# Gate logit as one more column of K's folded weight, and the skip diagonal made from the broadcast row

## Chip, cores and metric

The kernel runs on one core of one Trainium2 chip. The metric is device time in microseconds (us), the median of several executions. The kernel before was run three times: 148.78, 149.03 and 149.26 us, so its median is 149.03 us.

## What is computed

Two branches read the same input x (2048 tokens of 512 channels, bf16) and are mixed by a gate, one number a token. Branch A is a diagonal complex state-space recurrence of 512 states plus a skip term `x * Dskip`. Branch B is linear attention with 32 heads of 16 channels, whose features are softmaxes of a projected query or key and of its negative.

```python
    x = A_x
    g = _sigmoid((x * gate_w).sum(-1, keepdims=True))
    a = _A_ref(x, A_Lambda_re, A_Lambda_im, A_B_re, A_B_im, A_C_re, A_C_im, A_log_dt, A_Dskip)
    b = _B_ref(x, B_wqkv, B_w_phi, B_wo)
    return g * a + (1 - g) * b
...
        y = 2.0 * jnp.einsum("blp,dp->bld", hseq, Cmat).real + x * Dskip[None, None, :]
...
        pk = jnp.einsum("bhsd,hdf->bhsf", k, w_phi)
        phi_k = jnp.concatenate([_softmax(pk, axis=-1), _softmax(-pk, axis=-1)], axis=-1)
        kv = jnp.einsum("bhsf,bhsd->bhfd", phi_k, v)
```

## The kernel before

**The order of the work is written by hand.** Every stage is a generator (`st_k`, `st_a`, ...), and the list `ORDER` names them in turn: one token runs one generator up to its next `yield`. `@` gives the PSUM banks that a stage takes, `:D` gives an evacuation to the vector engine (DVE) in place of the scalar engine (ACT). Each engine then runs its own instructions in the order in which the tokens issued them, and a semaphore wait holds everything that stands behind it on that engine. So a token's place in the list is its place in the queue of every engine that it uses, GpSimd (POOL) and the DMA-issuing SP included.

**The prologue.** POOL makes a bf16 identity `ident`, issues the DMAs of the three parameter vectors into `vec_n` (L164), and makes an f32 identity `identf`, from which DVE builds masks (L283 to L288) and the block-diagonal `BD` of the feature weights (`st_B`, tokens `B`). TensorE (PE) transposes K's weight into `WTk` (`st_W`) and multiplies it by `BD`: that is the fold, `f0` to `f3`, one for each 128 input channels. Its evacuation writes K's folded weight `Wk2`, 480 columns (8 groups of 4 heads, 15 features a head: the first feature is the reference and stands as a zero). The products of a token tile with it (`k0` to `k15`, four matmuls each, L493) are evacuated by ACT into `Xq`, whose row for a tile is 8 groups of 64 elements, the first four of each zeroed by POOL (L279, L499).

**The parameters.** `V` transposes `vec_n` on PE and DVE casts it into `vec`. From there a long run of small DVE and ACT operations (tokens `U`, `P`, `M`) makes the recurrence's coefficients `dgs`. The last of them, `M2` (L421 to L429), runs on POOL: three of its operations and two in place (L424, L425) give the coefficients `S_NBI` and `S_BR`, L426 gives `S_NBR`, and L427 to L429 give powers of the decay. The stage `c` (L446 or L444, `C2<-CT,dgs`) multiplies the transposed C by these coefficients, on DVE for most tokens. `V2` is a second transpose, of `vec_m` (Dskip and gate_w, loaded by POOL at L281): DVE casts it into `vec`, POOL's `affine_select` (L339) makes from it the skip diagonal `Dd`, and `gw` makes a bf16 copy of gate_w, `gw_b`, on DVE (L398).

**The middle.** For each of five groups of token tiles DVE makes maxima, minima, differences and sums of features (`x`, `n`, `s`), ACT the exponentials (`e`), and PE accumulates the attention state (`a0` to `a4`, `st_a`). In the same `st_a` PE computes the gate's logit: for each of 16 tiles four matmuls with one column of output, `gw_b` against the token tile, into the unused end of a PSUM accumulator (L631). At the same time the state-space stages `b`, `g`, `z`, `h`, `H`, `p` run on all engines.

**The end.** `G` reads the logits and makes `nge` and the gate `G` (L803 to L809). The queries' features (`X0` to `X3`, `S0` to `S3`) go through SP's transposing DMAs into `phT` (L613), and PE then does, tile by tile, `y` (state-space output, L875, with the skip term by `Dd` at L882), `o` (L894) and `t` (the output projection, L943). `Drow`, Dskip broadcast to all partitions, is loaded by SP at L261 (token `Ld`) and used by four tiles whose skip term DVE makes (L913).

Of the kernel before, what the change touches and what calls it, by code (L numbers as in the profile page):

```python
# [27 lines left out]
k4@3 i0 M k2 i0 i0 i0 M Lb k10 i2 M k6 n0 k4 k7@0 k7 i2 Lb k8@7 i1 i2 x0 i1 i1 k13@6 M2 k11@0 n0 i2 k8 i1 x1 n1 x1 D  # L28
n1 x1 b200@1 i2 i1 L i0:D x1 D c1:D n1 Lc Lc i3:D n1 k11 e0 b010@7 b010 c0:D x1 n1 i2:D b200 x2 s0 c0:D s0 k12@3 k12
x2 g200@2 g200 n2 c1 b100@0 s0 b100 x2 b001@5 n2 Lv b000@7 Lc i1 b000 b111@4 b111 x2 n2 s0 n2 g000@2 b001 s0 c3:D  # L30
b011@3 b101@7 e1 x2 n2 g000 g000 Lx g001@5 g001 x3 s1 v1@4 b011 c3 s0 c2:D c2:D c1:D k14@2 g010@3 g010 Lo e2 x3 n3 s1
k13 D v0@0 v1 s1 g011@1 x3 c3:D g011 x3 g001 g011 v0 e2 k15@0 g011 g010 c0:D Lq Lq g010 s1 n3 k14 w2@6 c3 s0 D k15 n3
a0@54 s2 a0 g011 x3 n3 g011 Ld g010 g201@2 b101 Ld n3 s1 w2 g010 z0 b201@1 b201 z0 b110@7 n4 s1 x4 g101@3 g201 l2:D s2
s2 x4 n4 e3 z0 z0 w1@6 w1 b110 g100@2 g100 g101 g101 g100 s2 s2 s2 g111@1 l2:D l2:D g111 n4 g110@0 g110 e3 g110 g111
# [44 lines left out]
def kernel(  # L79
# [69 lines left out]
    vec_m = const.tile([8, P], BF16, name="vec_m")  # L149
# [13 lines left out]
    for n, src in enumerate((A_Lambda_im, A_Lambda_re, A_log_dt)):  # L163
        nc.gpsimd.dma_start(out=vec_n[4 * n:4 * n + 4, :], in_=src.rearrange("(j p) -> j p", p=P))  # L164

# [6 lines left out]
    gw_b = const.tile([P, KT], BF16, name="gw_b")  # L172
# [15 lines left out]
    Xq = pR.tile([P, NTI, D], BF16, name="Xq")  # L188
# [18 lines left out]
    WTk = Xq[:, 12:16, :]  # L207
# [71 lines left out]
    nc.gpsimd.memset(Xq[:, 0:12, :].rearrange("p n (hh x) -> p n hh x", hh=8)[:, :, :, 0:4], 0.0)  # L279
    for n, src in enumerate((A_Dskip, gate_w)):  # L280
        nc.gpsimd.dma_start(out=vec_m[4 * n:4 * n + 4, :], in_=src.rearrange("(j p) -> j p", p=P))  # L281
# [52 lines left out]
    def st_V2():  # L334
        pvt = bank([P, 8], BF16, "pvt")
        nc.tensor.transpose(pvt[:], vec_m[:], ident[0:8, 0:8])
        yield
        nc.vector.tensor_copy(out=vec[:, 3:5, :].rearrange("p n j -> p (n j)"), in_=pvt[:])
        nc.gpsimd.affine_select(out=Dd[:], in_=dsk.unsqueeze(2).to_broadcast([P, KT, P]), compare_op=ALU.is_equal,  # L339
                                fill=0.0, base=0, pattern=[[0, KT], [-1, P]], channel_multiplier=1)  # L340
        yield
# [55 lines left out]
    def st_gw():  # L397
        nc.vector.tensor_copy(out=gw_b[:], in_=vec[:, 4, :])  # L398
        yield

# [47 lines left out]
    def fold(W2, WT, dtile):  # L448
        pf = bank([P, DF], F32, "pf")
        for j in range(KT):  # L450
            MM(out=pf[:, j * DF // KT:(j + 1) * DF // KT], lhsT=WT[:, j, dtile * P:(dtile + 1) * P], rhs=BD[:, j].rearrange("p g f -> p (g f)"), start=True, stop=True)
        yield
        evac(W2[:, dtile, :].rearrange("p (hh f hl) -> p hh f hl", hh=8, f=Dh - 1), pf[:].rearrange("p (hh hl f) -> p hh f hl", hh=8, hl=4))
        yield

    def st_f(d):
        return fold(Wk2, WTk, d)

    def st_w(d):
        return fold(Wq2, WTq, d)  # L460
# [34 lines left out]
    def xrel(n):  # L495
        return Xq[:, n, :].rearrange("p (hh x) -> p hh x", hh=8)[:, :, 4:]

    def xzero(n0, n1):
        nc.gpsimd.memset(Xq[:, n0:n1, :].rearrange("p n (hh x) -> p n hh x", hh=8)[:, :, :, 0:4], 0.0)  # L499
# [5 lines left out]
    def st_k(ti):  # L505
        pk = bank([P, DF], F32, "pk")
# [27 lines left out]
    def v5(ap3):  # L534
        return ap3.rearrange("p l (hh f hl) -> p l hh f hl", hh=8, f=Dh)
# [14 lines left out]
    def feat_max(p, first, L):  # L550
        X5 = v5(Xq[:, first:first + L, :])
# [3 lines left out]
        VT(out=half(EE, 0), in0=X5, in1=live["mx", p].to_broadcast([P, L, 8, Dh, 4]), op=ALU.subtract)  # L555
        yield

    def feat_min(p, first, L):
        X5 = v5(Xq[:, first:first + L, :])
        yield from tree(X5, L, ALU.min, "mn", ("mn", p))  # L560
        VT(out=half(live["EE", p], 1), in0=live["mn", p].to_broadcast([P, L, 8, Dh, 4]), in1=X5, op=ALU.subtract)  # L561
        yield
# [56 lines left out]
    def st_a(n):  # L619
        first, L = KGROUPS[n]  # L620
        for u in range(L):
            n_ = first + u
            ti = KO[n_]
# [6 lines left out]
            for kt in range(KT):  # L630
                MM(out=live["acc"][1][:, 4 * KVW + ti:4 * KVW + ti + 1], lhsT=xT[:, kt, ti * P:(ti + 1) * P],  # L631
                   rhs=gw_b[:, kt:kt + 1], start=False, stop=(n_ == NTI - 1 and kt == KT - 1), skip_group_check=True)
# [329 lines left out]
    st = {"V": st_V(), "V2": st_V2(), "U": st_U(), "P": st_P(), "P2": st_P2(), "P3": st_P3(), "P4": st_P4(), "B": st_B(), "gw": st_gw(),  # L962
# [60 lines left out]
```

## Time and profile before

| | |
|---|---|
| three runs | 148.78, 149.03, 149.26 us; median 149.03 us |
| profiled execution, first to last instruction | 147.2 us span |
| what the median has beyond that span | 1.8 us |
| busy: PE, DVE, ACT, POOL | 140.8, 135.1, 123.4, 45.4 us |
| granted TensorE clock | full speed in all 40 slices |

The page names one time of the profiled execution, its span; its own total is taken as the span and the 1.8 us that the median has around it. Times below are positions in that span. In a timeline row the columns are start, duration, engine, line, operation, output and inputs, size, and in brackets the idle time just before with what ended it. A duration on DVE and ACT reaches a little into the next instruction, so the cost of one in a dense run is the distance between starts. PE's ends are modelled, so there too starts are what is compared. A DMA row on POOL or SP is the issue, not the transfer.

### The profile page before, as it was taken

Reading aid. Unit: us, or ns where it says so; the run is one execution under the profiler, and the core shown is the slowest. Engines: PE = TensorE matmul, PEld = TensorE weight load, DVE = VectorE, ACT = ScalarE, POOL = GpSimd, SP = SyncE. Lnnn points to the kernel's source line nnn. Section 1 sums busy time; section 2 is a strip of 40 time slices with the busy share of each in tenths; the row PEclk is TensorE's granted clock in tenths of the full one; section 3 lists DMA queues with packets and bytes.
Section 4 is the critical chain, followed back from the end, with each engine's and each line's share of the span. In section 5 each row is a group of like instructions: output and inputs, shape, how many; then the busy total and the mean of one; then the engine's idle time right before and its main releaser. Section 6 shows DMA issues by size and latency. Waiting matters only on the chain.

```text
span 147.2 us, 2881 instructions
## 1 busy us (share of the span) xinstructions
PE 140.8 (96%) x1014; PEld 73.3 (50%) x1014; DVE 135.1 (92%) x330; ACT 123.4 (84%) x222; POOL 45.4 (31%) x61
## 2 busy tenths in 40 slices
PE   6999999999999999999999999999979999999990
PEld 2744444444544644554454656545445554545650
DVE  2879999999999999999999999999998999979740
ACT  3479999999999999999999999999988997912110
POOL 7503600003138195797545353051003003000000
PEclk9999999999999999999999999999999999999999
DMA  5999998990846586789878969969988999999643
GB/s 123 233 184 170 181 179 160 239 290 2 195 94 90 88 114 99 80 127 169 131 111 141 144 90 191 123 126 164 208 179 153 192 214 159 199 180 271 129 111 114
DMA packets 56047, 22.63 MB, mean 154 GB/s; under 512 B 44768, under 2 KB 54880, under 8 KB 56032
## 3 DMA queue, kind: packets, MB, share of 16 engines
q1 hardware_dynamic: 47584, 15.05, 52.7%
q0 software_dynamic: 7504, 7.09, 33.8%
q10 hardware_dynamic: 944, 0.31, 0.9%
q8 instruction: 8, 0.13, 0.4%
q14 instruction: 7, 0.06, 0.1%
HBM read 2.51 MB, written 2.10 MB: 31 GB/s over the span
## 4 chain that ended last, share of the span: by engine, by line
DVE 45%; PE 36%; ACT 9%; DMA 4%; issue 3%; DVEq 0%
PE PS L875 17%; PE PS L943 8%; DVE EE L597 6%; DVE mn L544 5%; DVE mx L544 5%; DMA phT<-EE 4%; DVE EE L555 4%; DVE sq L575 4%; DVE EE L561 3%; PE PS L894 3%; PE PS L493 3%; PE PS L324 2%; DVE w L723 2%; ACT vx L137 2%; ACT Xq L137 2%
## 5 line engine op out<-in xcount | busy, mean ns | idle before, releaser
L567 ACT ACTIVATE EE<-EE 128x2048 bf16<-128x2048 bf16 x16 | 30.3, 1933 | 0.4 <-DVE EE L561 0.4
L493 PE MATMUL PS<-WKV,xT 128*128 128x480 bf16 (+1 forms) x128 | 29.2, 372 | 0.2 <-ACT WKV L137 0.2
L493 PEld LDWEIGHTS <-xT 128*128 128x128 bf16 x192 | 18.1, 97 | 19.7 <-issue 0.9
L137 ACT CAST Xq<-PS 128x480 bf16<-128x480 f32 x32 | 17.5, 592 | 0.2
L653 PE MATMUL PS<-xT,BT 128*128 128x512 bf16 x64 | 16.2, 379 | 0.0
L875 PE MATMUL PS<-C,H 128*128 128x512 bf16 x64 | 15.6, 379 | 0.0
L943 PE MATMUL PS<-Wo,oT 128*128 128x512 bf16 (+2 forms) x68 | 15.5, 366 | 0.0
L493 PE MATMUL PS<-Wq,xT 128*128 128x480 bf16 x64 | 14.9, 365 | 0.0
L641 PE MATMUL PS<-xT,BT 128*128 128x512 bf16 x64 | 14.8, 379 | 0.0
L529 POOL DMA_DIRECT2D C<-CT x4 | 6.8, 1712 | 18.1 <-DVE CT L446 18.1
L907 DVE TENSOR_TENSOR on<-PS,rd 128x512 bf16<-128x512 f32 x16 | 10.9, 684 | 1.0 <-ACT rd L901 0.9
L529 POOL DMA_DIRECT2D eb<-dg x4 | 4.8, 1201 | 22.3 <-ACT dg L444 10.9
L949 ACT ACTIVATE ot<-PS,G 128x512 bf16<-128x512 f32 (+1 forms) x10 | 6.3, 647 | 4.7 <-PE PS L943 4.7
L641 PEld LDWEIGHTS <-BT 128*128 128x128 bf16 x64 | 6.3, 98 | 7.5
L561 DVE TENSOR_TENSOR EE<-mn,Xq 128x2048 bf16<-128x2048 bf16 (+1 forms) x9 | 9.9, 1095 | 0.0
L555 DVE TENSOR_TENSOR EE<-Xq,mx 128x2048 bf16<-128x2048 bf16 (+1 forms) x9 | 9.8, 1094 | 0.0
L575 DVE TENSOR_TENSOR sq<-EE 128x2048 bf16<-128x2048 bf16 (+1 forms) x9 | 9.8, 1094 | 0.0
L943 PEld LDWEIGHTS <-oT 128*128 128x128 bf16 x68 | 6.4, 98 | 6.7
L898 ACT ACTIVATE ld<-PS 128x32 f32<-128x32 f32 x16 | 3.0, 202 | 7.8 <-PE PS L894 7.8
L597 DVE TENSOR_TENSOR EE<-EE,rc 128x2048 bf16<-128x2048 bf16 x8 | 9.6, 1210 | 0.0
L653 PEld LDWEIGHTS <-BT 128*128 128x128 bf16 x64 | 6.1, 97 | 6.9 <-issue 0.2
L137 ACT CAST vx<-PS 128x512 bf16<-128x512 f32 x16 | 9.5, 618 | 0.0
(196 smaller groups left out, 329.7 us busy)
## 6 DMA issues: line engine op xcount, KB each, us to landing
out_dram<-ot SPq DMA_DIRECT2D x7, 256.0 KB, 2.5
C<-CT POOLq DMA_DIRECT2D x4, 256.0 KB, 5.2
eb<-CT POOLq DMA_DIRECT2D x4, 256.0 KB, 4.3
eb<-dg POOLq DMA_DIRECT2D x4, 256.0 KB, 4.3
sq<-sq POOLq DMA_DIRECT2D x3, 256.0 KB, 3.8
WKV<-in_B_wqkv_dram SPq DMA_DIRECT2D x1, 512.0 KB, 4.9
Wo<-in_B_wo_dram SPq DMA_DIRECT2D x1, 512.0 KB, 4.1
WKV<-in_A_x_dram SPq DMA_DIRECT2D x2, 256.0 KB, 4.8
```

The costliest lines, as they stand in the source:

```text
L137: nc.scalar.copy(out=out_ap, in_=in_ap)
L493: MM(out=pt[:], lhsT=xT[:, kt, ti * P:(ti + 1) * P], rhs=W[:, kt, :], start=(kt == 0), stop=(kt == KT - 1))
L544: VT(out=dst, in0=cur[:, :, :, 0:n, :], in1=cur[:, :, :, n:2 * n, :], op=op)
L555: VT(out=half(EE, 0), in0=X5, in1=live["mx", p].to_broadcast([P, L, 8, Dh, 4]), op=ALU.subtract)
L561: VT(out=half(live["EE", p], 1), in0=live["mn", p].to_broadcast([P, L, 8, Dh, 4]), in1=X5, op=ALU.subtract)
L567: aexp(out=EE[:, l_:l_ + 2], in_=EE[:, l_:l_ + 2], func=ACT.Exp)
L575: VT(out=sq.rearrange("p q x i -> p x q i"), in0=e4[:, :, 0:2], in1=e4[:, :, 2:4], op=ALU.add)
L597: VT(out=E5[:, u:u + 2], in0=E5[:, u:u + 2], in1=rc[:, u:u + 2].to_broadcast([P, 2, 2 * NB, Dh, 4]), op=ALU.mult)
L641: MM(out=pb[:], lhsT=BT[:, ri, kt, j * P:(j + 1) * P], rhs=cells(kt, 2 * pr), start=(kt == 0), stop=(kt == KT - 1))
L653: MM(out=pgq[:], lhsT=BT[:, ri, kt, js], rhs=cells(kt, r1), start=(kt == 0), stop=(dst == 0 and j in LJ and kt == KT - 1))
L875: MM(out=py[:], lhsT=hs[j][ri], rhs=C2[:, 1 - ri, j, c:c + w], start=(j == 0 and ri == 0), stop=False)
L943: MM(out=py[:], lhsT=oT[:, g, :], rhs=Wo[:, g, c:c + w], start=False, stop=(g == HG - 1))
```

## The change

**The gate's logit becomes part of K's product.** The folded weight gets 61 columns a group in place of 60 (488 in all): the 61st column of the first group holds gate_w, those of the other seven are zeroed by a DVE memset at the start. `Xq` gets groups of 66 elements in place of 64, the 61 values of a group land at 4 to 64, and the logit of a token stands in element 64 of group 0. `G` reads it there. The 64 one-column matmuls of `st_a`, the `gw` stage and `gw_b` are gone.

**gate_w comes earlier.** Its DMA stands behind the three of `vec_n`, ahead of `identf`; the token `V2` stands ahead of `f3`, and its DVE copy writes straight into the folded weight.

**The skip diagonal is made from `Drow`.** Dskip's own small load is gone. A new stage `Dk` holds the `affine_select`, which now reads the row that SP's DMA broadcasts; its token stands behind `Ld`, the token that issues that DMA, and ahead of `M`, `M2` and `c`.

```diff
-W10:D f1:D T1@5 T1:D f2@3 f2 f3@0 f3:D k0@6 x0z:D Lx k1@7 V@3 V P U U k1 k1 k0 k0 P k3@3 P2 P P2 U P2 U k6@2 P2 P2 x0
-Lx Lb Lx Lb P4 n0 P4 k3 x0 V2@6 P4 V2 P3 i3 gw P2 n0 P3 k5@7 x0 i3 x0 Lc k5 k9@3 k9 i0 Ld k2@0 M n0 i3 i3 k10@1 i3
+W10:D f1:D T1@5 T1:D f2@3 f2 V2@1 V2 f3@0 f3:D k0@6 x0z:D Lx k1@7 V@3 V P U U k1 k1 k0 k0 P k3@3 P2 P P2 U P2 U k6@2 P2
+P2 x0 Lx Lb Lx Lb P4 n0 P4 k3 x0 P4 P3 i3 P2 n0 P3 k5@7 x0 i3 x0 Lc k5 k9@3 k9 i0 Ld Dk k2@0 M n0 i3 i3 k10@1 i3 k4@3 i0
...
-    vec_m = const.tile([8, P], BF16, name="vec_m")
+    vec_m = const.tile([4, P], BF16, name="vec_m")
...
-    Wk2, Wv = WKV[:, 0, :, 0:DF], WKV[:, 1]
+    KX = 8 * (4 * (Dh - 1) + 1)
+    Wk2, Wv = WKV[:, 0, :, 0:KX], WKV[:, 1]
+    Wk3 = Wk2.rearrange("p k (hh x) -> p k hh x", hh=8)
...
+    nc.vector.memset(Wk3[:, :, 1:8, DF // 8], 0.0)
...
+    nc.gpsimd.dma_start(out=vec_m[:], in_=gate_w.rearrange("(j p) -> j p", p=P))
...
-    Xq = pR.tile([P, NTI, D], BF16, name="Xq")
+    XW = 4 * Dh + 2
+    Xq = pR.tile([P, NTI, 8, XW], BF16, name="Xq")
...
-    for n, src in enumerate((A_Dskip, gate_w)):
-        nc.gpsimd.dma_start(out=vec_m[4 * n:4 * n + 4, :], in_=src.rearrange("(j p) -> j p", p=P))
...
     def st_V2():
-        pvt = bank([P, 8], BF16, "pvt")
-        nc.tensor.transpose(pvt[:], vec_m[:], ident[0:8, 0:8])
-        yield
-        nc.vector.tensor_copy(out=vec[:, 3:5, :].rearrange("p n j -> p (n j)"), in_=pvt[:])
-        nc.gpsimd.affine_select(out=Dd[:], in_=dsk.unsqueeze(2).to_broadcast([P, KT, P]), compare_op=ALU.is_equal,
+        pvt = bank([P, KT], BF16, "pvt")
+        nc.tensor.transpose(pvt[:], vec_m[:], ident[0:KT, 0:KT])
+        yield
+        nc.vector.tensor_copy(out=Wk3[:, :, 0, DF // 8], in_=pvt[:])
+        yield
+
+    def st_Dk():
+        nc.gpsimd.affine_select(out=Dd[:], in_=Drow[:].rearrange("p (k q) -> p k q", k=KT), compare_op=ALU.is_equal,
                                 fill=0.0, base=0, pattern=[[0, KT], [-1, P]], channel_multiplier=1)
         yield
...
-    def st_gw():
-        nc.vector.tensor_copy(out=gw_b[:], in_=vec[:, 4, :])
-        yield
...
-        evac(xrel(ti), pk[:].rearrange("p (hh x) -> p hh x", hh=8))
+        evac(xrel(ti, 4 * Dh + 1), pk[:].rearrange("p (hh x) -> p hh x", hh=8))
...
-            for kt in range(KT):
-                MM(out=live["acc"][1][:, 4 * KVW + ti:4 * KVW + ti + 1], lhsT=xT[:, kt, ti * P:(ti + 1) * P],
-                   rhs=gw_b[:, kt:kt + 1], start=False, stop=(n_ == NTI - 1 and kt == KT - 1), skip_group_check=True)
...
-        VS(out=nge[:], in0=live["acc"][1][:, 4 * KVW:4 * KVW + NTI], scalar1=-Z_MAX, scalar2=-1.0, op0=ALU.max, op1=ALU.mult)
+        VS(out=nge[:], in0=Xq[:, :, 0, 4 * Dh], scalar1=-Z_MAX, scalar2=-1.0, op0=ALU.max, op1=ALU.mult)
```

What this does to the engines' queues is shown at three places. The first is POOL's queue from the parameter DMAs to the coefficients of `M2`. Before, with each row's waits in brackets (`DMAHW` is a DMA issued by SP or ACT, `DMASW` one issued by POOL):

```order
L164 DMA vec_n<-in_A_log_dt_dram 4x128
masks.py:197 MEMSET identf 128x128
masks.py:199 AFFINE_SELECT identf<-identf 128x128 [waits Pool_49]
L278 IOTA iot 128x256
L279 MEMSET Xq 128x96x4
L281 DMA vec_m<-in_A_Dskip_dram 4x128
L281 DMA vec_m<-in_gate_w_dram 4x128
L499 MEMSET Xq 128x32x4 [waits DVE_49,PE_49,Activation_49]
L339 AFFINE_SELECT Dd<-vec 128x512 [waits DVE_49]
L421 TENSOR_TENSOR ssm_par<-dgs,vec 128x16 [waits DVE_49]
L422 TENSOR_TENSOR dgs<-ssm_par 128x4 [waits Pool_49]
```

And in the changed kernel:

```order
L166 DMA vec_n<-in_A_log_dt_dram 4x128
L167 DMA vec_m<-in_gate_w_dram 4x128
masks.py:197 MEMSET identf 128x128
masks.py:199 AFFINE_SELECT identf<-identf 128x128 [waits Pool_49]
L281 IOTA iot 128x256
L282 MEMSET Xq 128x96x4
L499 MEMSET Xq 128x32x4 [waits DVE_49,PE_49,Activation_49]
L343 AFFINE_SELECT Dd<-Drow 128x512 [waits DMAHW7_49]
L421 TENSOR_TENSOR ssm_par<-dgs,vec 128x16 [waits DVE_49]
L422 TENSOR_TENSOR dgs<-ssm_par 128x4 [waits Pool_49]
```

One DMA issue now stands ahead of `identf`, and the `affine_select`, still just ahead of `M2`, waits for a DMA of SP's where it waited for DVE.

The second place is DVE's queue where it reaches stage `c`; these rows are of the changed kernel, and the kernel before has the same rows in the same order with the same waits (`dg` is a set of diagonal matrices, `C_68` is `C2`, `mn` a tree of minima):

```order
L437 TENSOR_TENSOR dg<-ident,dgv 128x1536
L446 TENSOR_SCALAR C_68<-CT,dgs 128x512 [waits DMAHW6_49,DMAHW5_49,Pool_49]
L544 TENSOR_TENSOR mn<-mn 128x16x8
L446 TENSOR_SCALAR T2c<-T2c 128x256
L544 TENSOR_TENSOR mn<-mn 128x16x4 [waits DVE_49]
L446 TENSOR_SCALAR C_68<-CT,dgs 128x512 [waits DMAHW4_49]
```

Nothing moved here. The first multiplication by `S_BR` waits for POOL's `M2`, and all of DVE's later work stands behind it.

The third place is the prologue on DVE, from the last piece of `BD` to the cast of the parameters. Before (`WKV` holds the folded weight, `Xq` here `WTk`):

```order
L365 TENSOR_TENSOR BD<-Wd,mask_166 128x120
L139 COPY Xq<-PS 128x2x256 [waits PE_49]
L139 CAST WKV<-PS 128x480 [waits PE_49]
L139 COPY xT<-PS 128x4x128 [waits PE_49]
L139 CAST WKV<-PS 128x480 [waits PE_49]
L331 CAST vec<-PS 128x12 [waits PE_49]
```

And in the changed kernel:

```order
L369 TENSOR_TENSOR BD<-Wd,mask_165 128x120
L138 COPY Xq<-PS 128x2x256 [waits PE_49]
L138 CAST WKV<-PS 128x8x60 [waits PE_49]
L138 COPY xT<-PS 128x4x128 [waits PE_49]
L339 COPY WKV<-PS 128x4 [waits PE_49]
L138 CAST WKV<-PS 128x8x60 [waits PE_49]
L332 CAST vec<-PS 128x12 [waits PE_49]
```

The copy of gate_w (L339 of the changed kernel) has come in ahead of the evacuation of `f3`, and the first matmul of `k0` on PE, which waited for ACT's evacuation of `f0`, now waits for that copy. Farther down, the casts at L338 and L398 of the kernel before are gone from DVE.

More of the change, by code (lines that the diff above doesn't have):

```diff
@@ L30 @@
[L30 to L34, printed above, removed]
@@ L452, in fold @@
         yield
-        evac(W2[:, dtile, :].rearrange("p (hh f hl) -> p hh f hl", hh=8, f=Dh - 1), pf[:].rearrange("p (hh hl f) -> p hh f hl", hh=8, hl=4))
+        evac(W2[:, dtile].rearrange("p hh (f hl) -> p hh f hl", f=Dh - 1), pf[:].rearrange("p (hh hl f) -> p hh f hl", hh=8, hl=4))
         yield
     def st_f(d):
-        return fold(Wk2, WTk, d)
+        return fold(Wk3[:, :, :, 0:DF // 8], WTk, d)
     def st_w(d):
-        return fold(Wq2, WTq, d)
+        return fold(Wq2[:].rearrange("p k (hh x) -> p k hh x", hh=8), WTq, d)
     def st_i(j):
@@ L493, in tile_mm, with xrel @@
             MM(out=pt[:], lhsT=xT[:, kt, ti * P:(ti + 1) * P], rhs=W[:, kt, :], start=(kt == 0), stop=(kt == KT - 1))
-    def xrel(n):
-        return Xq[:, n, :].rearrange("p (hh x) -> p hh x", hh=8)[:, :, 4:]
+    def xrel(n, w=4 * Dh):
+        return Xq[:, n, :, 4:w]
     def xzero(n0, n1):
-        nc.gpsimd.memset(Xq[:, n0:n1, :].rearrange("p n (hh x) -> p n hh x", hh=8)[:, :, :, 0:4], 0.0)
+        nc.gpsimd.memset(Xq[:, n0:n1, :, 0:4], 0.0)
     def st_x0():
@@ L505, in st_k @@
     def st_k(ti):
-        pk = bank([P, DF], F32, "pk")
+        pk = bank([P, KX], F32, "pk")
         for h in range(2):
@@ L532, in half, with x5 @@
         return EE[:, :, :, sgn, :].rearrange("p l hh (f hl) -> p l hh f hl", f=Dh)
-    def v5(ap3):
-        return ap3.rearrange("p l (hh f hl) -> p l hh f hl", hh=8, f=Dh)
+    def x5(first, L):
+        return Xq[:, first:first + L, :, 0:4 * Dh].rearrange("p l hh (f hl) -> p l hh f hl", f=Dh)
     def tree(src5, L, op, nm, key, groups=NB):
@@ L550, in feat_max @@
     def feat_max(p, first, L):
-        X5 = v5(Xq[:, first:first + L, :])
+        X5 = x5(first, L)
         yield from tree(X5, L, ALU.max, "mx", ("mx", p))
@@ L558, in feat_min @@
     def feat_min(p, first, L):
-        X5 = v5(Xq[:, first:first + L, :])
+        X5 = x5(first, L)
         yield from tree(X5, L, ALU.min, "mn", ("mn", p))
```

52 lines of the change are left out of this document (27 added, 25 removed).

## The prediction

> **What bounds the kernel now.** The page comes first: its busy line and its chain of work that ended last.
>
> ```profile
> PE 140.8 (96%) x1014; PEld 73.3 (50%) x1014; DVE 135.1 (92%) x330; ACT 123.4 (84%) x222; POOL 45.4 (31%) x61
> ...
> DVE 45%; PE 36%; ACT 9%; DMA 4%; issue 3%; DVEq 0%
> ```
>
> PE and DVE are both nearly full, so neither share says what a saving on one is worth. The table by windows shows where each has room (window, length, then busy time of PE, PEld, DVE, ACT, POOL).
>
> ```profile
> 20.00:30.00 10.00, 10.00 (x48) 4.58 (x47) 10.00 (x28) 9.99 (x16) 0.00 (x0) 1.00 1.03 206
> ...
> 90.00:100.00 10.00, 9.99 (x105) 5.75 (x103) 10.00 (x26) 9.97 (x20) 2.40 (x2) 1.00 1.03 137
> 100.00:110.00 10.00, 8.94 (x73) 4.83 (x71) 9.93 (x22) 9.52 (x14) 0.00 (x0) 1.00 1.19 181
> ```
>
> Between 20 and 100 neither stands still. The first place where PE does is at 108.45, and three views tell why: the waits, the chain in order of time, and the timelines of DVE and PE.
>
> ```profile
> PE PS L894 <- DMA phT<-EE: 1.1, 1, 1.1
> ```
> ```profile
> 101.92 6.49 DMA phT<-EE
> 108.45 0.43 PE PS L894 x8
> ...
> 143.31 0.62 DVE ot L951
> ```
> ```profile
> 100.86 0.68 DVE L609 TENSOR_TENSOR EE<-EE,rho 128x1024 bf16<-128x1024 bf16 x1
> ```
>
> DVE's multiplication at L609 ends at 101.54, SP's transposing DMA takes its result from 101.92, and PE, idle for 1.1 us, goes on when that lands. From 108.45 to 143.3 the chain is PE alone. So the end is **DVE's dense run up to 101.54, plus the DMA, plus some 35 us of PE**. What DVE loses before 101.54 arrives at the end in full, because DVE has no idle time in which to make it good; what PE saves before 108.45 only makes its wait there longer. Everything that the change takes from PE lies before 91.1, as the next row shows.
>
> **What leaves PE.** By the view of the source line, with starts first and last, and PE's timeline at the first accumulation:
>
> ```profile
> L631 PE MATMUL PS<-gw_b,xT x64: 163/163/165, 37.7 to 91.1; 128*128 128x1 bf16 x64
> ```
> ```profile
> 37.67 0.24 PE L631 MATMUL PS<-gw_b,xT 128*128 128x1 bf16 x4
> 37.77 0.42 PE L627 MATMUL PS<-vx,EE 128*128 128x68 bf16 x8
> ```
>
> Four gate products occupy PE from 37.67 to 37.77, 25 ns each by distance of starts, whatever their durations say; 64 of them are 1.6 us. Against this, each of 64 matmuls of the `k` stages gets 8 more columns.
>
> ```profile
> 20.48 0.97 PE L493 MATMUL PS<-WKV,xT 128*128 128x480 bf16 x4
> 21.29 1.03 PE L653 MATMUL PS<-xT,BT 128*128 128x512 bf16 x4
> ```
>
> Four of 480 columns take 0.97 us, four of 512 take 1.03: 0.06 us for 128 columns, so 512 more columns cost 0.24 us. PE is 1.4 us better off, and by the argument above **the time gets nothing of it**: the work that hides it is DVE's.
>
> **ACT's evacuations.** 8 more elements in 16 of them, priced from these two rows of the page (480 and 512 elements, mean ns in the last column but the idle time):
>
> ```profile
> L137 ACT CAST Xq<-PS 128x480 bf16<-128x480 f32 x32 | 17.5, 592 | 0.2
> ...
> L137 ACT CAST vx<-PS 128x512 bf16<-128x512 f32 x16 | 9.5, 618 | 0.0
> ```
>
> 26 ns for 32 elements make 6.5 ns for 8, 0.1 us in all, most of it before 38 and beside a later DVE. I count nothing.
>
> **The prologue.** These are rows of the timelines of POOL, then DVE, then PE.
>
> ```profile
> 2.82 0.52 POOL L164 DMA_DIRECT2D vec_n<-in_A_log_dt_dram  x1
> ```
> ```profile
> 3.95 0.38 DVE L283 TENSOR_REDUCE M<-identf 128x4 f32<-128x128 f32 x1 [1.64 <-POOL identf masks.py:199]
> ...
> 8.92 0.17 DVE L331 CAST vec<-PS 128x12 f32<-128x12 bf16 x1 [0.58 <-PE PS L329]
> ...
> 11.65 0.16 DVE L338 CAST vec<-PS 128x8 f32<-128x8 bf16 x1
> ...
> 12.06 0.60 DVE L398 CAST gw_b<-vec 128x4 bf16<-128x4 f32 x1
> 12.57 0.28 DVE L544 TENSOR_TENSOR mn<-mn 128x256 bf16<-128x256 bf16 x1
> ```
> ```profile
> 7.80 0.97 PE L493 MATMUL PS<-WKV,xT 128*128 128x480 bf16 x4 [0.20 <-ACT WKV L137]
> 8.70 0.18 PE L329 MATMUL PS<-ident,vec_n 12*128 12x12 bf16 x1
> ```
>
> gate_w's DMA issue, 0.52 us like its neighbour, now stands ahead of `identf`, and DVE already waits 1.64 us for that: its masks, `BD` and the fold come 0.5 us later. The new V2 product waits for ACT's evacuation of `f0` (its bank), and `k0` for the copy of V2's result; the step from such a product to its cast is 0.22 us (8.70 to 8.92). I estimate the first `k0` matmul 0.65 us later, at 8.45, and with it the parameters' cast at 8.92. DVE then gets back the cast at 12.06 (0.51 us to the next start) and the one at 11.65 (0.08): at 20 us it is only **0.1 us later**.
>
> **The skip diagonal on POOL, the term that decides.** POOL's rows, then SP's, then the landing of that DMA:
>
> ```profile
> 11.89 0.75 POOL L339 TENSOR_SCALAR_AFFINE_SELECT Dd<-vec 128x512 bf16<-128x512 f32 x1 [3.96 <-DVE ssm_par L384]
> 13.98 0.33 POOL L421 TENSOR_TENSOR ssm_par<-dgs,vec 128x16 f32<-128x16 f32 x1 [1.34 <-DVE dgs L408]
> ...
> 15.37 0.21 POOL L425 TENSOR_TENSOR dgs<-dgs,ssm_par 128x8 f32<-128x8 f32 x1
> ...
> 16.57 0.78 POOL L429 TENSOR_TENSOR ssm_par<-ssm_par 128x4 f32<-128x4 f32 x1
> ```
> ```profile
> 15.87 0.58 SPq L261 DMA_DIRECT2D Drow<-in_A_Dskip_dram  x1
> ```
> ```profile
> DMA to landing us min/median/max: 4.4/4.4/4.4
> ```
>
> The `affine_select` has to wait for `Drow`, which lands at 15.87 + 4.4 = 20.3; SP's queue up to there is not changed. `M2` stands behind it on POOL, in order, though its own inputs are there at 14. Before, L421 to the end of L425 took 13.98 to 15.58, 1.6 us. And DVE needs L425's result here:
>
> ```profile
> 16.61 0.68 DVE L555 TENSOR_TENSOR EE<-Xq,mx 128x1024 bf16<-128x1024 bf16 x1
> ...
> 20.21 0.94 DVE L437 TENSOR_TENSOR dg<-ident,dgv 128x1536 bf16<-128x1536 bf16 x1
> 21.08 0.34 DVE L446 TENSOR_SCALAR C<-CT,dgs 128x512 bf16<-128x512 bf16 x1
> ```
>
> With nothing in POOL's way, L425 ends at 20.3 + 0.75 + 1.6 = 22.65, and with 0.1 us for the semaphore DVE's 21.08 becomes 22.75: 1.7 us. But POOL and DVE hold each other up. L429 took 0.78 us where its like took 0.2 to 0.4, and ended at 17.35 just behind the two-input L555 (17.29); the cast of four elements at 12.06 took 0.60 and ended at 12.66 with the `affine_select` (12.64). `dg`, 0.87 us from start to start, has two inputs in memory and starts at 20.3, just as `Drow` lands, so it comes into POOL's way or POOL into its. All of it in series adds 0.87 (2.5 us in all), and the other bound is POOL's operations without the stretching that they had before (0.4 less, 1.3 us). I take half of `dg`: **2.1 us**. This contains the 0.1 us of the prologue, since the wait is for a DMA whose time is fixed.
>
> The Trainium skill ("SBUF — State Buffer", § Who interferes with whom) has the second port that VectorE and GpSimd share as an exclusive lock, which a DVE operation with two SBUF inputs takes against a GpSimd one that reads. The two rows at 12.06 and 16.57 agree with it. By that rule alone the sum would be the full 2.5 us, 151.5.
>
> Queued behind the waiting DVE instruction is all that DVE does to the end. PE waits for it first at `a0` (37.41), then at 108.45, and ACT at the exponentials. The profiled execution's span of 147.2 becomes 149.3; with the 1.8 us that the median has around the span, the time is **149.03 + 2.1 = 151.1 us**. The `G` stage's new source is 16 elements, the memset at the start lies in DVE's wait for `identf`: nothing for both.
>
> **Rivals.**
> 1. *The wait does not bind.* If `Drow` lands 2 us sooner, or stage `c` needs `M2` later than its row says, only the prologue's 0.1 us is left: 149.1. Against it, the transfer's time is a row, and the queue order names POOL among the waits at 21.08.
> 2. *PE sets the end after all, and the kernel gets faster.* The saving of 1.4 us would be seen if PE's stream, 96% busy, decided: 147.6. It decides only if DVE reaches L609 earlier than 101.54, for the 1.1 us of PE's wait are DVE's; and DVE gets only 0.6 us back while the prologue takes 0.65.
> 3. *The longer rows of `Xq` slow DVE.* A group now starts every 132 bytes. If that made the reading dearer by one part in eight, which I take as the upper bound since the last two rows show no loss at all, these groups, 9.8 and 9.9 us, would take 2.5 us more on top of the forecast: 153.6.
>
> ```profile
> L561 DVE TENSOR_TENSOR EE<-mn,Xq 128x2048 bf16<-128x2048 bf16 (+1 forms) x9 | 9.9, 1095 | 0.0
> L555 DVE TENSOR_TENSOR EE<-Xq,mx 128x2048 bf16<-128x2048 bf16 (+1 forms) x9 | 9.8, 1094 | 0.0
> ```
> ```profile
> L759 DVE TENSOR_TENSOR mc<-mc,H x2: 400/410/421, 82.3 to 86.8; 128x512 bf16<-128x512 bf16 x2
> L727 DVE TENSOR_TENSOR H<-w,T2c x2: 405/408/410, 49.0 to 58.2; 128x512 bf16<-128x512 bf16 x2
> ```
>
> Against it, L759 reads `H` from an offset of 4 bytes and takes what L727 takes on its aligned inputs (410 and 408 ns); nothing excludes a small gain either. The Trainium skill (same page, § Specifications (TRN2)) has 16-byte lines and a penalty for each line crossed, with two hits a line needed for full rate; rival 3 would follow from that rule, and no row of the trace has groups of 132 bytes.
>
> **How the numbers follow.** DVE waits for `M2` behind `Drow`: 0.80, from 150.3 (1.3 us) to 151.9 (2.9: all of `dg`, and 0.4 more of such stretching). Rival 1: 0.08. Rival 2: 0.05. Rival 3: 0.05. Else 0.02. The range goes from 149.6 to 152.3, so that the two rivals below and most of the third stay out. A measurement of this kernel can tell about 0.3%, 0.45 us, from no change. Faster 0.05, same 0.09, slower 0.86.
>
> **What would show it.** POOL's `affine_select` starts near 20.4 instead of 11.89, its idle time ended by the DMA of `Drow`. DVE's first `C<-CT` starts at 22.4 to 24.0 instead of 21.08 and shows POOL L425 as what it waited for. DVE's wait for `identf` grows from 1.64 to about 2.2. PE's `a0` starts some 2 us later than 37.41. Between `a0` and the `phT` wait PE has 1.4 us less to do in the same length of DVE's work, so its idle time there grows by about that, most of it at `phT`. If DVE does not wait at `C`, the sum is wrong at its largest term; if DVE waits there and L609 comes less than that later, the claim that DVE has no room is wrong; if the groups on `Xq` are longer than 1095 ns, rival 3 holds.

## The result, and the profile after

The changed kernel takes 151.59 us (median of five runs, 151.29 to 152.12), the kernel before 149.24 beside it: a ratio of **1.0173, 95% interval 1.0149 to 1.0197** (ratios, here and below, come from all runs of both kernels, so they differ a little from the quotient of the two medians). The forecast was 151.1, the range 149.6 to 152.3. The profiled execution has a span of 149.9 us, 2.7 more than before, with PE's work smaller:

```profile
PE 140.1 (94%) x950; PEld 71.8 (48%) x950; DVE 135.3 (90%) x330; ACT 123.5 (82%) x222; POOL 45.7 (30%) x60
```

**The wait at C is there.** POOL's timeline after, then DVE's:

```profile
19.64 1.13 POOL L343 TENSOR_SCALAR_AFFINE_SELECT Dd<-Drow 128x512 bf16<-128x512 bf16 x1 [10.83 <-DMA Drow<-in_A_Dskip_dram]
20.75 1.01 POOL L421 TENSOR_TENSOR ssm_par<-dgs,vec 128x16 f32<-128x16 f32 x1
```
```profile
20.18 0.63 DVE L544 TENSOR_TENSOR mx<-mx 128x64 bf16<-128x64 bf16 x1
20.74 0.95 DVE L437 TENSOR_TENSOR dg<-ident,dgv 128x1536 bf16<-128x1536 bf16 x1
22.78 0.35 DVE L446 TENSOR_SCALAR C<-CT,dgs 128x512 bf16<-128x512 bf16 x1 [1.10 <-POOL dgs L425]
```

The `affine_select` sat 10.83 us until `Drow` came, and DVE's first multiplication of C starts at 22.78 where it started at 21.08: 1.70 us later, 1.10 of it a plain wait for L425. Most of the rest is in the row of `mx`, which in the kernel before reads:

```profile
20.11 0.18 DVE L544 TENSOR_TENSOR mx<-mx 128x64 bf16<-128x64 bf16 x1
```

From `mx` to the next start DVE took 0.10 us before and 0.56 now, while the `affine_select` ran; and the `affine_select` took 1.13 us in place of 0.75, L421 1.01 in place of 0.33.

**The end is later by more than that.** DVE stays 1.7 us behind up to the multiplication at L609, and the transpose of its result is issued at 103.66 (SP's timeline), 1.74 later than before. But PE is only 0.50 late at the product that waited for it (108.45 before), and then 2.60 late at the next place (117.06 before):

```profile
103.66 2.50 SPq L613 DMA_TRANSPOSE phT<-EE  x1
```
```profile
108.96 0.32 PE L890 MATMUL PS<-KVm,phT 128*128 128x68 bf16 x5
```
```profile
113.34 6.27 DMA oT<-on
119.61 0.05 issue
119.66 1.90 PE PS L939 x8
```
```profile
PE PS L939 <- DMA oT<-on: 1.6, 1, 1.6
```

The third piece is from the chain in order of time, the last from the waits. The row of the kernel before at this place has no wait:

```profile
117.06 1.89 PE L943 MATMUL PS<-Wo,oT 128*128 128x512 bf16 x8
```

The wait for `phT` (1.1 us before) is gone, and a wait for `oT`, the transposed normalised output, has come: its transfer is issued 1.72 us later than before (113.34 after 111.62) and takes 6.27 us where it took 5.0. What stretches a transfer shows in the windows of 1 us (length, busy PE, PEld, DVE, ACT, POOL, clock, DMA share, GB/s; the share counts a packet whole in the window where it starts, so it can exceed 1). First the kernel before, then the changed one:

```profile
105.00:106.00 1.00, 1.00 (x7) 0.46 (x5) 1.00 (x3) 1.00 (x2) 0.00 (x0) 1.00 1.12 207
106.00:107.00 1.00, 1.00 (x6) 0.42 (x5) 1.00 (x4) 1.00 (x1) 0.00 (x0) 1.00 2.78 144
107.00:108.00 1.00, 0.40 (x5) 0.21 (x3) 1.00 (x6) 1.00 (x2) 0.00 (x0) 1.00 0.06 6
```
```profile
106.00:107.00 1.00, 1.00 (x6) 0.45 (x5) 1.00 (x4) 1.00 (x1) 0.00 (x0) 1.00 1.16 216
...
117.00:118.00 1.00, 1.00 (x7) 0.29 (x3) 1.00 (x2) 1.00 (x1) 0.00 (x0) 1.00 2.74 46
118.00:119.00 1.00, 0.07 (x1) 0.00 (x0) 1.00 (x3) 1.00 (x2) 0.00 (x0) 1.00 0.10 12
```

Hardly any packet starts, before at 107 (6 GB/s) and after at 117 to 119 (46, 12). The DMA queues of the windows in which this begins, 106 to 107 of the kernel before and 116 to 117 of the changed one:

```profile
q1 hardware_dynamic: 508, 0.13, 272.1%
q8 instruction: 1, 0.02, 5.8%
```
```profile
q1 hardware_dynamic: 452, 0.11, 177.7%
q8 instruction: 1, 0.02, 10.7%
```

Each holds one packet of the instruction queue, 0.02 MB. There are 8 such packets in the kernel before and 7 in the changed one, for 2028 and 1900 matmul and weight-load instructions: about one for each 256. They are refills of PE's instruction stream. The one of the first pair starts at 106.39 and lasts 0.93 us (5.8% of 16 x 1 us), to 107.32; within it there is a stretch in which no packet of any queue starts:

```profile
106.75:107.29 0.54, 0.54 (x6) 0.31 (x4) 0.54 (x4) 0.54 (x1) 0.00 (x0) 1.00 0.00 0
```

In the whole window from 106 to 107 the transposes' packets in the kernel before took 86 ns each (2.721 x 16 us over 508), against 22 ns (1.159 x 16 over 844) in the same window of the changed kernel, which has no refill there:

```profile
q1 hardware_dynamic: 844, 0.22, 115.9%
```

Taking 64 products away took 128 instructions from PE's stream and so moved the refills. The one that had met `phT` now meets `oT`. The Trainium skill ("Runtime: NRT & Kernel Launch", § Instruction fetch mechanics) has refills in blocks of 256 instructions and calls their cost mostly hidden; the count agrees, but the transfers beside them are not undisturbed here.

### The profile page after: what moved, and what is told of

Its sections match the earlier page's. It is cut to its first block, busy times and chain, and to the rows that moved or that the text cites. A ratio compares the mean times of both kernels' runs of the same rounds, so it can differ in the third digit from the quotient of the medians.

```text
span 149.9 us, 2750 instructions
## 1 busy us (share of the span) xinstructions
PE 140.1 (94%) x950; PEld 71.8 (48%) x950; DVE 135.3 (90%) x330; ACT 123.5 (82%) x222; POOL 45.7 (30%) x60
## 4 chain that ended last, share of the span: by engine, by line
PE 34%; DVE 30%; ACT 12%; SPq 10%; DMA 7%; issue 3%; POOL 2%; DVEq 0%
PE PS L871 16%; PE PS L939 9%; SPq L235 6%; DMA oT<-on 4%; DVE mn L544 4%; DVE EE L555 3%; DVE mx L544 3%; DVE EE L597 3%; DVE EE L561 3%; DVE sq L575 3%; PE PS L890 3%; DMA Drow<-in_A_Dskip_dram 3%; ACT EE L567 2%; ACT vx L136 2%; SPq L241 2%
## 5 line engine op out<-in xcount | busy, mean ns | idle before, releaser
L493 PE MATMUL PS<-WKV,xT 128*128 128x488 bf16 (+1 forms) x128 | 29.4, 374 | 0.3 <-ACT H L136 0.2
L136 ACT CAST Xq<-PS 128x488 bf16<-128x488 f32 (+1 forms) x32 | 17.5, 592 | 0.2
L575 DVE TENSOR_TENSOR sq<-EE 128x2048 bf16<-128x2048 bf16 (+1 forms) x9 | 10.0, 1107 | 0.0
```

The source lines that it names most:

```text
L136: nc.scalar.copy(out=out_ap, in_=in_ap)
L493: MM(out=pt[:], lhsT=xT[:, kt, ti * P:(ti + 1) * P], rhs=W[:, kt, :], start=(kt == 0), stop=(kt == KT - 1))
L575: VT(out=sq.rearrange("p q x i -> p x q i"), in0=e4[:, :, 0:2], in1=e4[:, :, 2:4], op=ALU.add)
```

## Experiments

Two theories were put against each other. **D**: DVE's wait at C is the whole loss, and what PE has to do before the last waits for transposes costs or brings nothing. **R**: besides that wait, where PE's refills meet the transposes decides about another 1 us in either direction. The waits in the table are PE's in each profiled execution, that at C is DVE's, in us. The waits for `phT` in e2, e6, e8 and e11 are for the transfer before the one near 108. Ratios are to the kernel before, run beside each.

| kernel | median us | ratio, 95% interval | at C | phT | oT |
|---|---|---|---|---|---|
| before | 149.24 | 1 | 0 | 1.1 | 0 |
| changed | 151.59 | 1.0173 (1.0149 to 1.0197) | 1.1 | 0 | 1.6 |
| e1 | 150.94 | 1.0115 (1.0086 to 1.0143) | 0 | 0 | 1.6 |
| e2 | 152.44 | 1.0207 (1.0170 to 1.0244) | 1.7 | 0.7 | 0 |
| e3 | 150.53 | 1.0079 (1.0046 to 1.0112) | 1.1 | 1.1 | 0 |
| e4 | 149.62 | 1.0036 (1.0008 to 1.0065) | 0 | 0 | 1.5 |
| e5 | 151.17 | 1.0143 (1.0117 to 1.0170) | 1.7 | 1.0 | 0 |
| e6 | 150.54 | 1.0112 (1.0085 to 1.0140) | 1.7 | 0.2 | 0.3 |
| e7 | 149.49 | 1.0042 (1.0017 to 1.0066) | 0 | 0 | 0 |
| e8 | 148.89 | 0.9991 (0.9968 to 1.0014) | 0 | 0.9 | 0 |
| e9 | 150.25 | 1.0075 (1.0047 to 1.0102) | 0 | 0 | 0.6 |
| e10 | 149.29 | 1.0027 (1.0014 to 1.0040) | 0 | 1.0 | 0 |
| e11 | 149.01 | 1.0000 (0.9982 to 1.0017) | 0 | 0.7 | 0 |
| e12 | 149.73 | 1.0074 (1.0042 to 1.0106) | 0 | 0 | 0.9 |

### The wait: e1, e3, e9

**e1** keeps the changed kernel and puts the `affine_select` behind `M2`.

```diff
-Ld Dk k2@0 M ... k13@6 M2 k11@0
+Ld k2@0 M ... k13@6 M2 Dk k11@0
```

> The changed kernel with the token Dk moved behind M2, so that POOL makes the coefficients before it waits for Drow. Theory D (DVE's wait at C is the whole loss, and PE only follows): DVE's first C<-CT is back at about 21.3, L609 ends where it did before, and the time is 149.3 us, the time before. Theory R (besides DVE's wait, a 16 KB refill of PE's instructions, which moved with the 128 fewer PE instructions from 106.4 to 116.4 us, holds up the transposing DMAs of the outputs): DVE is back as in D, but the refill near 115 still meets a transfer of oT or phT, and 0.8 to 1.3 us of the loss stay: 150.1 to 150.6 us.

150.94 us: the wait at C is gone, and 0.6 us with it (0.9 by the ratios), less than either theory had. POOL's row, DVE's near C and one farther on, and PE's longest wait for a transfer:

```profile
19.74 1.25 POOL L343 TENSOR_SCALAR_AFFINE_SELECT Dd<-Drow 128x512 bf16<-128x512 bf16 x1 [2.08 <-DMA Drow<-in_A_Dskip_dram]
```
```profile
20.41 0.62 DVE L544 TENSOR_TENSOR mx<-mx 128x64 bf16<-128x64 bf16 x1
20.95 0.95 DVE L437 TENSOR_TENSOR dg<-ident,dgv 128x1536 bf16<-128x1536 bf16 x1
...
69.54 0.49 DVE L446 TENSOR_SCALAR CT<-H,dgs 128x1024 bf16<-128x1024 bf16 x1 [0.37 <-DMA C<-CT]
```
```profile
PE PS L939 <- DMA oT<-on: 1.6, 1, 1.6
```

The `affine_select` still runs at 19.7 beside `mx`, which costs DVE 0.54 us to the next start where 0.10 was usual, so DVE is 0.74 us behind the kernel before at C. At 69.54 it waits 0.37 us for a DMA, which neither the kernel before nor the changed one shows there (e2, e6 and e7 do, 0.3 to 0.4 us); why that DMA comes late stays open. So DVE is still 1.2 us behind at L609, and the wait for `oT` is as long as in the changed kernel. D, which had everything back, falls.

**e3** makes only this part of the change in the kernel before: `Dd` from `Drow`, in a stage `Dk` behind `Ld`; PE's stream stays as it was.

```diff
-        nc.gpsimd.affine_select(out=Dd[:], in_=dsk.unsqueeze(2).to_broadcast([P, KT, P]), compare_op=ALU.is_equal,
...
+    def st_Dk():
+        nc.gpsimd.affine_select(out=Dd[:], in_=Drow[:].rearrange("p (k q) -> p k q", k=KT), compare_op=ALU.is_equal,
...
```

> The kernel before with only the skip diagonal's source and place changed (made from Drow, token Dk behind Ld as in the changed kernel); the gate's 64 products stay. Theory D: DVE's first C<-CT comes 1.7 us later, and so does everything: 150.9 to 151.1 us. Theory R: DVE's wait is the same, but PE's refill is as many instructions into its stream as before, comes near 108 and meets the phT transfer later in its course or not at all, so that less than the 1.7 us arrives at the end: 149.7 to 150.7 us.

150.53 us, 1.2 above the kernel before by the ratio (1.0079 of 149.2), inside R's range and below D's. DVE waits 1.1 us for POOL at C and starts there at 22.64, PE waits 1.1 us for `phT` as in the kernel before, and nowhere for `oT`. So this part of the change alone has about half of the loss.

**e9** leaves the order as changed and loads `Drow` early, by POOL.

```diff
-        nc.sync.dma_start(out=Drow[:], in_=A_Dskip.partition_broadcast(P))
...
     nc.gpsimd.memset(Xq[:, 0:12, :, 0:4], 0.0)
+    nc.gpsimd.dma_start(out=Drow[:], in_=A_Dskip.partition_broadcast(P))
```

> The changed kernel (151.59 us) with the DMA of Drow issued by POOL behind the memset of Xq, where Dskip's small load had stood, instead of by SP in the token Ld; the token Dk stays where it is. Drow should land near 9 to 10 us and the affine_select end before 13. D: DVE's wait for M2 at C (1.1 us, 1.7 us later) goes, and with it the whole loss: 149.1 to 149.4. R: the wait at C goes too, but PE's stream is still without the 64 products, so a refill stands near 114 to 115 and the wait of 1.5 us for oT stays: 149.6 to 150.1, as with e4 (149.62).

150.25 us, beyond both theories' numbers but with R's picture. Rows of POOL's timeline and of DVE's:

```profile
10.23 0.64 POOL L343 TENSOR_SCALAR_AFFINE_SELECT Dd<-Drow 128x512 bf16<-128x512 bf16 x1 [1.39 <-DMA Drow<-in_A_Dskip_dram]
```
```profile
10.27 0.62 DVE L374 TENSOR_SCALAR ssm_par<-ssm_par 128x4 f32<-128x4 f32 x1
...
20.63 0.18 DVE L544 TENSOR_TENSOR mx<-mx 128x64 bf16<-128x64 bf16 x1
20.73 0.95 DVE L437 TENSOR_TENSOR dg<-ident,dgv 128x1536 bf16<-128x1536 bf16 x1
21.60 0.34 DVE L446 TENSOR_SCALAR C<-CT,dgs 128x512 bf16<-128x512 bf16 x1
```

The `affine_select` is done before 11, `mx` takes 0.18 us, and DVE does not wait at C. The collision has moved rather than gone: beside the `affine_select` DVE's L374, four elements, takes 0.62 us, where it took 0.17 in the changed kernel. Of the 0.52 us by which DVE is late at C about 0.4 comes from there; the prologue itself had left 0.13 in the changed kernel. Yet 0.75% is left of the loss of 1.73%. The seven runs lie at 149.46 to 149.62 (three) and 150.25 to 150.67 (four); the profiled one is of the lower three, so its wait of 0.6 us for `oT` may be less than the usual one.

### PE's stream: e4, e2, e5, e6, e8, e12

**e4** takes the 64 gate products out of the kernel before. One product with unrelated weights writes the 16 logits instead, so this kernel leaves the gate out.

```diff
-            for kt in range(KT):
-                MM(out=live["acc"][1][:, 4 * KVW + ti:4 * KVW + ti + 1], lhsT=xT[:, kt, ti * P:(ti + 1) * P],
-                   rhs=gw_b[:, kt:kt + 1], start=False, stop=(n_ == NTI - 1 and kt == KT - 1), skip_group_check=True)
+            if n_ == NTI - 1:
+                MM(out=live["acc"][1][:, 4 * KVW:4 * KVW + NTI], lhsT=xT[:, 0, 0:P],
+                   rhs=warm[:, 0:NTI], start=False, stop=True, skip_group_check=True)
```

> The kernel before with 64 of the gate's products left out (one product of 16 columns with unrelated weights writes the 16 logits, so the gate is not computed). Nothing else is changed: no DVE, POOL or DMA order. Theory D: PE is 1.6 us better off before 91 and waits that much longer for phT: 149.2 us, no change. Theory R: the refill that stood at 106.4 moves by 126 instructions to near 115, so the phT wait gets shorter and a wait for oT appears near 117: between 148.5 and 150.2 us, with PE's longest wait in another place. A rival that PE's stream sets the end: 147.6 us.

149.62 us, 0.36% slower (0.08 to 0.65) with less work; the profiled execution, 150.09, is one of its slower ones (148.80 to 150.89). The wait for `phT` is gone and `oT` is late, as in the changed kernel; its transfer in the chain, and the queue in the window from 115 to 116:

```profile
111.95 6.18 DMA oT<-on
```
```profile
q8 instruction: 1, 0.02, 9.9%
```

DVE does not wait at C here. It is 0.34 us behind the profile of the kernel before from 8.9 on, long before the first edited product (37.7), and so are e8 and e12 (0.35 and 0.32); this is no effect of the edit. PE is 1.12 us late at `oT` (118.18), most of it from the transfer, which took 5.0 us before. So the wait for `oT` comes from PE's shorter stream and not from the wait at C. The rival that PE's saving would show in full (147.6) is out.

**e2** tried to move the refills by cutting each warm-up product in four.

```diff
-            MM(out=pz[:], lhsT=warm[:, 0:P], rhs=warm[:], start=True, stop=True)
+            for c in range(0, D, 128):
+                MM(out=pz[:, c:c + 128], lhsT=warm[:, 0:P], rhs=warm[:, c:c + 128], start=True, stop=True)
```

> The changed kernel with each of the eight warm-up products of 512 columns cut in four of 128 (their results are not used): 48 more PE instructions at the start, the same columns. Every later refill of PE's instructions comes 48 instructions, some 3 us, sooner: near 113 instead of 116.4, where SP has no transpose in flight. Theory D: nothing changes, 151.6 us. Theory R: PE's wait for oT near 119.7 goes from 1.6 to below 0.5 us, and the time is 150.0 to 150.6 us.

152.44 us: a miss of both. The wait for `oT` went, but DVE got a new one (its waits, then the chain):

```profile
DVE w L720 <- DMA mc<-ms: 1.4, 1, 1.4
```
```profile
54.36 5.36 DMA mc<-ms
```
```profile
q8 instruction: 1, 0.02, 9.6%
```

The last row is the instruction queue from 57 to 58: a refill now fell into the transfer of `mc`, for which DVE waits. In the thirteen other traces the same transfer has no refill in it and takes 3.4 us. Moving all refills moved one into a worse place.

**e5** puts 64 products of zeros where the gate's had stood.

```diff
+            for kt in range(KT):
+                MM(out=live["acc"][1][:, 4 * KVW + n_:4 * KVW + n_ + 1], lhsT=warm[:, 0:P],
+                   rhs=warm[:, 0:1], start=False, stop=(n_ == NTI - 1 and kt == KT - 1), skip_group_check=True)
```

> The changed kernel with 64 one-column products of zeros put back into st_a, four behind each tile, where the gate's products had stood; nobody reads their column. Nothing else differs from the changed kernel (151.59 us). D, the wait at C is the whole loss and PE's work before the last feature transpose costs nothing: 151.6, as without them. A plain count of PE's work: 1.6 us more, up to 153.2. R, a 16 KB refill of PE's instruction stream that meets a transposing DMA holds it up: the refills go back to their places of the kernel before (one near 108, none from 113 to 120), the wait for oT (1.6 us) goes, the wait for phT (about 1 us) comes back, and the time falls to 150.4 to 150.9 although PE does more.

151.17 us, between the two theories, and its interval overlaps that of the changed kernel: the time alone decides nothing here. The trace does. The picture of the kernel before is back, 1.9 us later from C to the end (waits, then chain):

```profile
PE PS L893 <- DMA phT<-EE: 1.0, 2, 0.8
```
```profile
103.82 6.41 DMA phT<-EE
```

**e6** puts 24 such products into the fourth group only.

```diff
+            for _ in range(6 if n == 3 else 0):
+                MM(out=live["acc"][1][:, 4 * KVW + 16:4 * KVW + 17], lhsT=warm[:, 0:P],
+                   rhs=warm[:, 0:1], start=False, stop=False, skip_group_check=True)
```

> The changed kernel with 24 one-column products of zeros in the fourth group of st_a (six behind each of its tiles), so that the last refills come 48 instructions earlier. By the matmuls' starts in the changed kernel's trace the refill at 116.4 moves to about 113.6, where no transpose has packets under way (111.7 to 115.0), the one at 98.6 to about 96.4 and the one at 135.9 to about 133.7. R: no wait of more than 0.3 us for oT, and 149.7 to 150.3 us. D: 151.6, the same as without them.

150.54 us, 1.05 below the changed kernel (0.9 by the ratios) with more work, the intervals apart. D falls here; R's range ended 0.24 us lower. PE's wait for `oT`:

```profile
PE PS L942 <- DMA oT<-on: 0.3, 1, 0.3
```

**e8** is e4 with the edit of e6; it leaves the gate out too.

> The kernel of e4 (the kernel before without the 64 gate products, the gate not computed; 149.62 us, its trace shows a wait of 1.5 us for oT) with the 24 products of zeros of e6. D: 149.2 to 149.6, PE's work there is hidden either way. R: the wait for oT goes and PE's saving before the end is seen: 147.9 to 148.5.

148.89 us, again between the two. `oT` is in time, but another refill met the transpose before (from the chain), and PE waited 0.9 us for that:

```profile
90.03 9.29 DMA phT<-EE
99.32 0.05 issue
99.36 0.43 PE PS L897 x8
```

**e12** adds 36 products (`range(9 if n == 3 else 0)`) to the kernel before.

> The kernel before (149.07 us) with 36 products of zeros added in the fourth group of st_a, nine behind each tile, 0.9 us of PE's work. By the starts of the kernel before the refill at 106.4 moves to about 100.5, into the stretch from 97.5 to 102 in which no transpose has packets, the one at 123.4 to about 118.5. D, products before the phT wait cost nothing: 149.1. A plain count of PE's work: up to 150.0. R: the transpose of phT issued near 102 takes about 5 us instead of 6.5 and PE's wait of 1.1 us goes: 148.1 to 148.7, faster with more work.

149.73 us: R's number is missed by 1 us, and the plain count of PE's work (up to 150.0) comes nearest. The wait for `phT` did go, as R had it, but two waits for `oT` came, and PE was 1.3 us late behind the added products at 84. How much of the 0.9 us is the work itself and how much the new waits is not settled.

### Both parts: e7, e10, e11

**e7** is e1 and e6 together, with the DMA of gate_w issued behind `identf`.

```diff
-    nc.gpsimd.dma_start(out=vec_m[:], in_=gate_w.rearrange("(j p) -> j p", p=P))
...
     make_identity(nc, identf[:])
+    nc.gpsimd.dma_start(out=vec_m[:], in_=gate_w.rearrange("(j p) -> j p", p=P))
```

> Three edits of the changed kernel at once: the token Dk behind M2 (as in e1), the gate_w DMA issued behind identf instead of ahead of it, and the 24 products of zeros of e6. D: the first two give back DVE's wait at C and the 0.5 us of the prologue, the third nothing, so 149.2 (the kernel before) to 149.5, at best. R: moreover no wait of PE for phT or oT is left, and the 1.4 us that PE saves arrive in part: 147.9 to 148.7, faster than the kernel before.

149.49 us, at the end of D's range. Neither transfer is late, yet PE's saving does not arrive: R expected too much. DVE reaches `dg` 0.6 us later than in the kernel before, the hold-up of e1 among it, and is 1.0 us late behind the wait near 69 that e1 has too.

**e10** is e9 with the products of e5, **e11** is e9 with those of e6.

> e9 and the 64 products of zeros of e5: Drow early, and PE's stream as long as in the kernel before. D: as e9, 149.1 to 149.4. R: no wait for oT, about 1 us for phT, 0.4 us below e9 as e5 stands below the changed kernel: 149.1 to 149.6.

> e9 and the 24 products of zeros of e6: Drow early, and the last refills some 48 instructions earlier, by e7's trace near 94.5, 111 and 130. D: as e9, 149.1 to 149.4. R: no wait above 0.3 us for oT or for the phT near 108: 148.3 to 149.0, below the kernel before (149.07).

149.29 us fits both; 149.01 is 0.01 above R's range and 0.09 below D's. R had e11 below the kernel before, which it is not, and its trace has a wait of 0.7 us for the `phT` before the one near 108. In e10 the picture of the kernel before is back (the chain; in the window from 106 to 107 stands a refill):

```profile
102.39 6.41 DMA phT<-EE
```

The six kernels make a table of two independent edits:

| ratio | no product of zeros | 64 | 24 |
|---|---|---|---|
| `Drow` by SP, as changed | 1.0173 | 1.0143 | 1.0112 |
| `Drow` early | 1.0075 | 1.0027 | 1.0000 |
| worth of loading early | 0.98% | 1.16% | 1.12% |

Loading `Drow` early is worth 1.5 to 1.7 us whatever PE's stream is, and the products of zeros are worth 0.3 to 0.75% whatever `Drow` does (the 0.30% of e5 is not clear of the noise). Within the noise the two causes add up. e11 beats the changed kernel by 1.7% and cannot be told from the kernel before; no version beat that one.

What is shown: the wait behind `Drow`, put into the kernel before by e3, and taken away in two ways, behind `M2` (e1, e7) and by the early load (e9 to e11); and that the length of PE's instruction stream decides which transfer is late, since products that nobody reads move the waits.

That a refill itself holds the transfers up rests on coincidence in time, but on a close one in all 14 traces. The `phT` issued between 101.9 and 105.7 took 6.4 to 6.5 us in the four with a refill within it (before, e3, e5, e10) and 4.4 to 4.8 us in the ten without. The `oT` issued between 111.6 and 115.6 took 6.2 to 6.3 us in the changed kernel, e1 and e4, each with a refill, and 4.3 to 5.5 us in the ten without; in e9 one falls into it and it takes 5.30 us, so not every meeting costs the same. In those seven long transfers there is a stretch of 0.3 to 0.7 us without the start of any packet, and it ends within 0.02 us of the end of the refill's packet, wherever the edit put that. Why a packet of 16 KB stops 16 DMA engines stays open, as does a way to say beforehand what a shift is worth: e2, e8 and e12 missed.

## Why the prediction was right, point by point

**The forecast's main mechanism was right and its place too. That the sum is right within 0.5 us is partly luck, since two errors of opposite sign met in it.**

- *The wait for `M2` behind `Drow`*: taken as 2.1 us, it was 1.70 in the trace, and 1.5 to 1.7 us by e9 to e11. Two terms in it were off and partly cancelled. `Drow` landed at 15.71 + 3.86 = 19.6 and not at 20.3, 0.7 less. POOL and DVE in each other's way stretched POOL's work from the start of the `affine_select` to the end of L425 to 3.11 us (19.64 to 22.75) where 2.35 were counted: 0.76 more, and not half of `dg`, 0.43. Two rows took 1.06 more (1.13 and 1.01 where 0.75 and 0.33 were counted), the four behind them 0.3 less. The step from L425 to DVE took 0.03 and not 0.1. The Trainium skill ("SBUF — State Buffer", § Who interferes with whom) with its exclusive lock had made this term the whole of `dg`, 0.87. The trace's 0.76 lies nearer to that than to the half. Of the two rows that the forecast set beside this rule, the cast at 12.06 has one input, as L374 of e9 has: both show the hold-up, but not that two inputs are its condition.
- *DVE has no room to make it good*: right. DVE is 1.7 us behind at every start from 22.8 to 110.
- *What PE saves only makes its wait at `phT` longer, and counts nothing*: **this step failed.** The 1.1 us there were the refill's and not DVE's. The transfer of `phT` took 6.49 us with a refill in it; without one it takes 4.76 (103.66 to 108.42 in the changed kernel). Taking the products away moved that refill, so PE came out only 0.50 late at `phT`; with 6.49 us again it would have been 1.7. It came out 2.60 late at `oT`, where the refill then stood: that transfer was issued 1.72 later, took 1.2 us longer, and in the kernel before had landed 0.4 us before PE came to it. The net, about 0.9 us (2.6 less 1.7), was missing from the sum. e4 shows the same without any wait at C, at 0.36% of loss. Nor did PE's idle time grow at `phT`: it grew earlier, by 1.9 us between 20 and 100, 1.05 of it from 30 to 40 (where `a0` waits for DVE, 39.13 after 37.41).
- *The prologue*: identf 0.5 us later (DVE's wait for it 2.01, forecast about 2.2), `k0` at 8.43 (forecast 8.45), and 0.13 us late at 12.57 (forecast 0.1). Since the wait at C is for a DMA, none of it counts in the changed kernel. In e9 to e11, without that wait, DVE is 0.4 to 0.6 us late there, but 0.34 to 0.45 of it is the hold-up beside the `affine_select` near 10.3; only the rest is the prologue's.
- *Longer rows of `Xq`*: priced at nothing, rightly. Its two groups of instructions after, and one that does not read `Xq`:

```profile
L561 DVE TENSOR_TENSOR EE<-mn,Xq 128x2048 bf16<-128x2048 bf16 (+1 forms) x9 | 9.9, 1105 | 0.0
L575 DVE TENSOR_TENSOR sq<-EE 128x2048 bf16<-128x2048 bf16 (+1 forms) x9 | 10.0, 1107 | 0.0
L555 DVE TENSOR_TENSOR EE<-Xq,mx 128x2048 bf16<-128x2048 bf16 (+1 forms) x9 | 9.9, 1105 | 0.0
```

All three are about 1% longer than before (L575 had 1094 ns too), so the 132 bytes have no part in it, and the third rival is out.

## What to carry to other kernels

A load that feeds a small operation on an otherwise idle engine is on the critical path as soon as an in-order queue has something urgent behind it: here moving one operand from values that were there at 12 us to a row that lands at 19.6 cost 1.5 to 1.7 us, and issuing that load early gave it back. Before taking a wait for a transfer as the lateness of its source, compare the transfer's duration with its like: 6.5 us against 4.8 said that the transfer itself had been held up, and its windows show what was under way beside it. And taking instructions out of a long stream shifts the refills behind them, so differences of about half a per cent from such an edit should be tested by putting idle instructions back.

## What the runs showed of the hardware

- A refill of PE's instruction stream (one packet of 16 KB for about 256 instructions) can go along with a pause of nearly all DMA traffic: 6 GB/s from 107 to 108 in the kernel before, 46 and 12 from 117 to 119 in the changed one, where 207 and 216 stand just before. A transpose that it met took up to 1.7 us longer (6.49 against 4.8).
- DVE and POOL hold each other up in both directions: the `affine_select` takes 0.64 us in e9 and 1.13 to 1.25 in the changed kernel and e1, and beside it a DVE maximum of 64 columns takes 0.62 to 0.63 us in place of 0.18, and a DVE operation on four elements 0.62 (e9) in place of 0.17.
